# Attention scores as one native float32 product instead of three products of two-part splits

## The chip, the cores and the metric

The kernel runs on one core of a Trainium2 chip. It has five engines with a queue of instructions each: TensorE (PE, with its weight loads listed as PEld), VectorE (DVE), ScalarE (ACT), GpSimd (POOL) and SyncE (SP, which only issues transfers). An engine works through its queue in order; engines wait for each other by semaphores. The metric is the device time of one execution in microseconds (us).

## The reference

Three stages follow each other, all in float32, for 2 sequences of 768 tokens. The change is in the first, attention with 8 heads of 64 columns:

```python
scores = scale * np.matmul(q, k.transpose(0, 1, 3, 2))
keep = is_global | is_local          # the first 8 keys, and the last 96 up to the query
scores = np.where(keep, scores + bias, -1e9)
a = np.exp(scores - np.max(scores, axis=-1, keepdims=True))
a = a / (np.sum(a, axis=-1, keepdims=True) + 1e-09)
x = np.matmul(a, v)
```

The second mixes over the sequence by a product of rank 32 (`moe_U`, `moe_V`) and runs a two-layer channel network with 2048 hidden columns. The third sends each token to one of 8 experts (512 to 1024 to 512) and weights the result. The weights of the second stage come as float64.

## The kernel before, in words

Attention works on 16 heads (2 sequences of 8), two heads (a pair) in the two halves of the 128 partitions. A head has 6 steps, one for each 128 queries, so there are 96 steps, z = 0 to 95. A step's window of keys is 256 columns wide: the local ones and a copy of the first 32.

TensorE multiplies in two ways here. For a tile of type float32r an instruction is one pass over the columns. A product of plain float32 tiles (native, here `values`) is one instruction in the program, and shows as two records in the profile, each with its own weight load. In order to get float32 accuracy from passes, q and k are split into a high part and the rest: kh and kl, qh and ql. `scores` (line 344) then adds three products: kh qh, kl qh, kh ql (lines 351 to 353). A head's q stands in its own half of the partitions and zeros in the other half, so the other head's keys drop out of the sum.

`split_pair` (line 124) makes these parts: for k a cast (line 133) and a subtraction (line 134), for q a cast (139) and a subtraction (140). The first pair is split in two halves of columns ahead of the loop, k on VectorE and q on ScalarE and GpSimd. Each later pair is split while the one before it runs, at the 3rd, 5th and 7th of that pair's 12 steps (`SPLITS`, counted from 0), k's subtraction and both of q's on GpSimd. `load_pair` (line 101) brings raw q and k for a pair, one buffer each, from step 8 of the pair two before on.

A step z is put into the queues in this order: the scores of z; the transposes of step z - 3 (line 376) and their copy on ScalarE (378); the softmax of z, that is one instruction on VectorE that adds the bias and gives the row minimum m (line 363) and an exponential on ScalarE (367); the value products of step z - 6 (392 to 395). There are two score buffers, so the scores of z wait until VectorE is through with those of z - 2. At a head's end VectorE divides by the sums (399 to 401).

One further piece of work is put into the queues with each step, in a fixed order by z (`bg`, `fill`): constants of the mixing stage, then the conversion of the first channel weights from float64 (`from_f64`, lines 230 to 237: four VectorE instructions, one a step), and from step 55 on the mixing product and the transposes of the first sequence. GpSimd also makes a head's bias (line 213, for five of the heads). SyncE issues the transfers in program order; it stops at one whose buffer isn't free.

After step 54 all engines pass a branch around the general form of attention (`other_windows`), and again after the loop. Then come the channel products and the experts, which the change doesn't touch.

Of the kernel before, what the change touches and what calls it, by code (L numbers as in the profile page):

```python
# [22 lines left out]
P = 128  # L23
# [14 lines left out]
# smallest normal float32, as the square of a float64's high word read as float32  # L38
# [3 lines left out]
# positions: the rest of the expert with two tiles or more so far, then the others by falling  # L42
# count in this order; tiles of tokens for each, more are taken at the end
# [9 lines left out]
SPLITS = (3, 5, 7)  # L53
BG0, BGR, SM0 = 6, 8, 6
# columns of the routing's tables
# [9 lines left out]
def tile_kernel(ctx, tc, q, k, v, nn, U, V, w12, wg, wgt, ew, masks, lst0, out, dbg=None):  # L65
# [24 lines left out]
    # ---------------------------------------------------------------- attention: loads  # L90
# [8 lines left out]
    raw_t, qk_t = {}, {}  # L99

    def load_pair(n, parts=1):
        """two heads, one in each half of the partitions"""
        b, h = heads[2 * n]
        if n == 0:
            qr, kr = (x_all[1][:, c:c + 2].rearrange("p a d -> p (a d)")[:, :w] for c, w in ((1, S), (3, NT * 160)))
        else:
            qr = ap.tile([P, S], F32, tag="qr", bufs=1, name=f"qr{n}")
            kr = ap.tile([P, NT * 160], F32, tag="kr", bufs=1, name=f"kr{n}")
        for c in range(parts):
            for t, src in ((kr, k), (qr, q)):  # L110
                w = t.shape[1] // parts
                nc.sync.dma_start(t[:, c * w:c * w + w], src[b, h:h + 2].rearrange("h d s -> (h d) s")[:, c * w:c * w + w])
        raw_t[n] = qr, kr

    # columns: 1, first head, second head, 1; the ones give the sums of the weights
# [5 lines left out]
    # q's parts of one head, zeros in the other head's half of the partitions  # L121
    q_parts = [[[ap.tile([P, S], F32R, name=f"q{w}{j}{r}", bufs=1) for w in "hl"] for j in range(2)] for r in range(2)]

    def split_pair(n, parts=1):
        """q and k in two parts each, whose products sum to float32's"""
        qr, kr = raw_t.pop(n)
        qs = q_parts[n % 2]
        kh = ap.tile([P, NT * 160], F32R, tag="kh", name=f"kh{n}")
        kl = ap.tile([P, NT * 160], F32R, tag="kl", name=f"kl{n}")
        qk_t[n] = qs, kh, kl  # L130
        def k_part(c):
            kc = slice(c * NT * 160 // parts, (c + 1) * NT * 160 // parts)
            nc.vector.tensor_copy(kh[:, kc], kr[:, kc])  # L133
            (nc.vector if parts > 1 else nc.gpsimd).tensor_tensor(kl[:, kc], kr[:, kc], kh[:, kc].bitcast(F32), ALU.subtract)  # L134

        def q_part(c, j):
            qc, r = slice(c * S // parts, (c + 1) * S // parts), slice(D * j, D * j + D)
            hi, lo = qs[j][0][r, qc], qs[j][1][r, qc]
            (nc.scalar.copy if parts > 1 or j == 1 else nc.vector.tensor_copy)(hi, qr[r, qc])
            nc.gpsimd.tensor_tensor(lo, qr[r, qc], hi.bitcast(F32), ALU.subtract)  # L140

        k_part(0)
        q_part(0, 0)
        yield
        for c in range(1, parts):
            k_part(c)
            q_part(c, 0)
            yield
        for c in range(parts):
            q_part(c, 1)  # L150
            yield

    # ---------------------------------------------------------------- constants
# [5 lines left out]
    nc.scalar.dma_start(msk, masks[:, P:7 * P])  # L159
    one_act = const.tile([1, 1], F32, name="one_act")  # L160
    nc.gpsimd.memset(one_act, 0.0)
    nc.scalar.activation(one_act, one_act, AF.Exp)
    nc.sync.dma_start(ident, masks[:, :P])
# [5 lines left out]
    for t in q_parts[0][0]:  # L169
        nc.vector.memset(t[D:].bitcast(F32), 0.0)  # L170
# [3 lines left out]
    first_split = split_pair(0, 2)  # L174
    run(first_split)

    for t in q_parts[1][0]:
        nc.scalar.copy(t[D:], q_parts[0][0][0][D:].bitcast(F32))
# [11 lines left out]
    def distance(dst, is_l, is_g, t, rel, gidx):  # L190
        """dst: the distance where kept, 0 elsewhere; t: 1 where kept"""
        nc.vector.tensor_scalar(is_l, rel, 0.0, None, ALU.is_ge)
        nc.vector.scalar_tensor_tensor(is_l, rel, nlf, is_l, ALU.is_lt, ALU.mult)
        nc.vector.tensor_scalar(is_g, gidx, ngf, None, ALU.is_lt)
        nc.vector.tensor_tensor(t, is_l, is_g, ALU.max)
        nc.vector.tensor_tensor(is_g, t, is_l, ALU.subtract)
        nc.vector.tensor_tensor(dst, rel, is_l, ALU.mult)
        nc.vector.scalar_tensor_tensor(dst, is_g, nlf, dst, ALU.mult, ALU.add)

    # the distance, far where masked; a head's bias is -8 x its slope x this  # L200
# [15 lines left out]
    run(first_split)  # L216
    for t in q_parts[0][1]:
        nc.gpsimd.memset(t[:D].bitcast(F32), 0.0)
    drain(first_split)
    for r in range(2):  # L220
        for c in (0, P + 1):
            nc.gpsimd.memset(v_two[r][:, :, c:c + 1], 1.0)
    for t in q_parts[1][1]:
        nc.gpsimd.memset(t[:D].bitcast(F32), 0.0)

    def from_f64(dst, sq, raw):
        """dst (float32) from the words of float64 in raw [p, n, 2]; below float32's range: zero"""
# [12 lines left out]
    # ---------------------------------------------------------------- weights of the channel products  # L240
    # room for the two parts of two chunks: two of them in "hl"; the float64 words' place, later a third; a fourth at the end
# [39 lines left out]
    # ---------------------------------------------------------------- mixing constants  # L281
# [33 lines left out]
    # routing constants  # L315
# [19 lines left out]
    # ---------------------------------------------------------------- attention: steps  # L335
# [8 lines left out]
    def scores(z):  # L344
        n, i = steps[z]
        k0 = 32 if i == 0 else 160 * (i - 1) + 64
        qs, kh, kl = qk_t[n // 2]
        qh, ql = qs[n % 2]
        c, kc = slice(P * i, P * i + P), slice(k0, k0 + 256)
        s = psa.tile([P, 512], F32, tag="s", bufs=2, name=f"s{z}")  # L350
        nc.tensor.matmul(s[:, :256], qh[:, c], kh[:, kc], start=True, stop=False)  # L351
        nc.tensor.matmul(s[:, :256], qh[:, c], kl[:, kc], start=False, stop=False)  # L352
        nc.tensor.matmul(s[:, :256], ql[:, c], kh[:, kc], start=False, stop=True)  # L353
# [49 lines left out]
    def whole_rows(b, gp):  # L403
        """attention over whole rows, for any n_global and n_local"""
# [66 lines left out]
    # ---------------------------------------------------------------- mixing over the sequence  # L471
    ut = {}

    def mixing(b):
        """x + V'(U'x), in parts: U's and x's first, then those of V and of the product"""
# [49 lines left out]
    # ---------------------------------------------------------------- attention: the loop  # L525
# [6 lines left out]
    spl = first_split  # L532
    for z in range(total + LAGV):
        if z < total:
# [7 lines left out]
            if z == 1:  # L542
                drain(spl)
            if i == 1 and 0 < n + 1 < H:
                head_bias(n + 1)
            if zz == SPLITS[-1] + 1 and n // 2 + 2 < len(heads) // 2:
                drain(spl)
                load_pair(n // 2 + 2)
            if zz in SPLITS and n // 2 + 1 < len(heads) // 2:
                if zz == SPLITS[0]:  # L550
# [854 lines left out]
```

## Time and profile before

| | |
|---|---|
| median of 3 runs | 671.55 us (668.97 to 677.45) |
| span of the profiled execution, first to last instruction | 671.4 us |
| TensorE / VectorE / ScalarE / GpSimd busy | 608.3 / 452.8 / 305.8 / 206.3 us |
| score products, first and last start of line 351 | 8.0 and 144.8 us |
| mean granted TensorE clock | 0.957 of full |

The profiled execution's own time is its span of 671.4 us; no other time was taken of it. Busy time counts what an engine executes, not what it waits for, and overlapping matmuls once. The granted clock is 1.00 (2.4 GHz) or 0.50 (1.2 GHz) at a moment; numbers between are means over a stretch.

### The profile page before, as it was taken

What the parts mean: (1) busy time and instruction counts of PE and PEld (TensorE: products, weight loads), DVE (VectorE), ACT (ScalarE), POOL (GpSimd) and SP (SyncE); (2) the same over time, 40 slices, a digit from 0 to 9 for tenths busy, and PEclk for the clock granted to TensorE, in tenths of its full rate; (3) what the DMA queues carried; (4) which work ended last, traced back from release to release, by engine and by line L of the source; (5) the groups of instructions that cost most, each with busy time, mean ns of one, the idle gap of its engine ahead of it and who ended that gap; (6) DMA issues with size and microseconds to landing.
All of it is one profiled execution on the core that took longest, in us unless ns stands there. A gap on an engine that the chain in (4) does not pass through costs nothing. (4 is left out here: it accounts for less than half of the span.)

```text
span 671.4 us, 10019 instructions
## 1 busy us (share of the span) xinstructions
PE 608.3 (91%) x3568; PEld 541.6 (81%) x3568; DVE 452.8 (67%) x1001; ACT 305.8 (46%) x644; POOL 206.3 (31%) x143
## 2 busy tenths in 40 slices
PE   5989768987998999999999799798989999999991
PEld 3888767986887999989998688776778988889891
DVE  7888959755888887145999651756663568685840
ACT  4766656864333333233222121632353567585830
POOL 4755425602033333223333352502351124031101
PEclk8987978998999999999999899899899999999997
DMA  9632635200333230033010001716257485967300
GB/s 247 226 99 91 213 112 197 65 3 3 125 126 126 93 131 27 0 126 126 32 48 1 0 2 56 289 47 142 95 183 304 146 278 175 364 257 287 125 12 27
DMA packets 35801, 84.08 MB, mean 125 GB/s; under 512 B 5567, under 2 KB 17727, under 8 KB 33680
## 3 DMA queue, kind: packets, MB, share of 16 engines
q1 hardware_dynamic: 31568, 71.52, 31.2%
q0 software_dynamic: 2784, 7.09, 3.0%
q10 hardware_dynamic: 1376, 4.59, 1.8%
q8 instruction: 33, 0.54, 0.4%
q14 instruction: 40, 0.33, 0.2%
HBM read 75.32 MB, written 8.77 MB: 125 GB/s over the span
## 5 line engine op out<-in xcount | busy, mean ns | idle before, releaser
L609 ACT ACTIVATE hh<-g 128x384 fp32r<-128x384 f32 x62 | 30.4, 490 | 115.0 <-PE g L606 114.6
L610 DVE SCALAR_TENSOR_TENSOR hl<-g,hh 128x384 fp32r<-128x384 f32 x62 | 34.2, 554 | 51.8 <-ACT hh L609 51.5
L367 ACT ACTIVATE e<-t,m 128x256 f32<-128x256 f32 (+1 forms) x96 | 47.3, 493 | 31.4 <-DVE m L363 30.6
L351 PE MATMUL s<-kh,qh 128*128 128x256 f32 x96 | 38.0, 396 | 23.6 <-DVE m L363 17.5
L848 POOL DMA_INDIRECT out_dram<-x,ids x13 | 13.1, 1008 | 123.8 <-ACT x L847 100.2
L363 DVE CUSTOM_DVE_ANT_0 t<-s,bias 128x256 f32<-128x256 f32 (+1 forms) x96 | 37.4, 394 | 17.9 <-PE s L353 11.5
L677 DVE CUSTOM_DVE_ANT_0 sq_w<-x,wgt 128x512 f32<-128x512 f32 x54 | 46.3, 857 | 1.4
L230 ACT ACTIVATE sq_w<-w 128x512 f32<-128x512 f32 x32 | 21.5, 671 | 49.7 <-DVE wf L237 49.7
L351 PEld LDWEIGHTS s<-kh,qh 128*128 128x128 f32 x96 | 20.5, 214 | 27.8 <-DVE m L363 21.4
L378 ACT COPY et<-pt 128x256 f32<-128x256 f32 (+1 forms) x96 | 33.2, 347 | 13.6 <-PE pt L376 12.8
L376 PE MATMUL pt<-ident,e 128*128 128x128 f32 x176 | 38.0, 292 | 0.0
L235 DVE SCALAR_TENSOR_TENSOR wf<-w,wf 128x512 int32<-128x512 int32 x32 | 35.2, 1100 | 0.8
L134 POOL TENSOR_TENSOR kl<-kr,kh 128x960 fp32r<-128x960 f32 x7 | 21.6, 3081 | 43.8 <-DVE kh L133 25.4
L395 PE MATMUL o<-v,et 128*128 128x65 f32 x160 | 33.6, 295 | 0.0
L768 POOL DMA_INDIRECT lst<-tab,slot x12 | 12.8, 1063 | 65.7 <-DVE tab L764 31.3
L233 DVE SCALAR_TENSOR_TENSOR wf<-w,wf 128x512 int32<-128x512 int32 x32 | 29.0, 908 | 4.6 <-issue 4.1
L610 DVE SCALAR_TENSOR_TENSOR ehlr<-egr,ehhr 128x256 fp32r<-128x256 f32 x28 | 11.9, 425 | 26.8 <-ACT ehhr L609 26.8
L353 PE MATMUL s<-kh,ql 128*128 128x256 f32 x96 | 29.4, 306 | 0.0
L352 PE MATMUL s<-kl,qh 128*128 128x256 f32 x96 | 29.4, 306 | 0.0
L394 PE MATMUL o<-v,et 128*128 128x65 f32 x160 | 29.0, 266 | 0.0
L140 POOL TENSOR_TENSOR ql<-qr,qh 64x768 fp32r<-64x768 f32 x14 | 26.9, 1918 | 1.4 <-POOL ql L140 1.0
L395 PEld LDWEIGHTS o<-v,et 128*128 128x128 f32 x160 | 27.0, 211 | 0.0
(777 smaller groups left out, 2150.4 us busy)
## 6 DMA issues: line engine op xcount, KB each, us to landing
ew<-in_ew_dram SPq DMA_DIRECT2D x32, 1024.0 KB, 7.5
w<-in_w_dram SPq DMA_DIRECT2D x16, 1024.0 KB, 4.8
v<-in_v_dram SPq DMA_DIRECT2D x8, 704.0 KB
ew<-in_ew_dram ACTq DMA_DIRECT2D x4, 1024.0 KB, 14.3
kr<-in_k_dram SPq DMA_DIRECT2D x7, 480.0 KB
x2d<-x SPq DMA_DIRECT2D x12, 256.0 KB
qr<-in_q_dram SPq DMA_DIRECT2D x7, 384.0 KB, 3.0
wgt<-in_wgt_dram SPq DMA_DIRECT2D x4, 512.0 KB, 3.6
```

The lines of the kernel that those rows point to most:

```text
L235: nc.vector.scalar_tensor_tensor(t, high, -0x40000000, t, ALU.bitwise_and, ALU.bitwise_or)
L351: nc.tensor.matmul(s[:, :256], qh[:, c], kh[:, kc], start=True, stop=False)
L352: nc.tensor.matmul(s[:, :256], qh[:, c], kl[:, kc], start=False, stop=False)
L353: nc.tensor.matmul(s[:, :256], ql[:, c], kh[:, kc], start=False, stop=True)
L363: nc.vector.tensor_tensor_reduce(out=t[:, :w], in0=s[:, :w], in1=bias[:, h, b0:b0 + w], scale=-0.125, scalar=3.0e38, op0=ALU.add, op1=ALU. ...
L367: nc.scalar.activation(e[:, :w], t[:, :w], AF.Exp, bias=m, scale=-1.0)
L376: nc.tensor.transpose(pt[:, c0:c0 + P], e[:, c0:c0 + P], ident)
L378: nc.scalar.copy(et[:, :w], pt[:, :w])
L395: nc.tensor.matmul(oo, et[:, P:256], vt[:, i, vc], start=False, stop=True)
L609: nc.scalar.activation(hi, src, AF.Relu)
L610: nc.vector.scalar_tensor_tensor(lo, src, 0.0, hi.bitcast(F32), ALU.max, ALU.subtract)
L677: nc.vector.tensor_tensor_reduce(out=sq_w, in0=x_t[0, i], in1=rooms[k % 2][:, DM * j:DM * j + DM], scale=1.0, scalar=0.0, op0=ALU.mult, op ...
```

## The change

Raw k goes into `kt`, two buffers in turn, and q straight into two tiles for each of two pairs in turn, a head's 64 rows in its half of the partitions; the other half is cleared once at the start. Both stay plain float32. `scores` is one native product. `split_pair`, the four part tiles and `SPLITS` are gone. A pair's loads are now issued at the second step of the pair before it (in the first pair's case at the start, as before), in three transfers instead of two. The transfer of the identity moves from SyncE's queue to ScalarE's, and the ones beside v are written earlier. Comments are removed, so line numbers differ.

```diff
-    raw_t, qk_t = {}, {}
+    qk_t = {}
+    q_two = [[ap.tile([P, S], F32, name=f"q{j}{r}", bufs=1) for j in range(2)] for r in range(2)]
+    def q_zero(r, engine):
+        for j in range(2):
+            engine.memset(q_two[r][j][D * (1 - j):D * (1 - j) + D], 0.0)
     def load_pair(n, parts=1):
         b, h = heads[2 * n]
-        ...
-                nc.sync.dma_start(t[:, c * w:c * w + w], src[b, h:h + 2].rearrange("h d s -> (h d) s")[:, c * w:c * w + w])
-        raw_t[n] = qr, kr
+        kt = ap.tile([P, NT * 160], F32, tag="kt", bufs=2, name=f"kt{n}")
+        qk_t[n] = q_two[n % 2], kt
+        def k_part(c):
+            w = NT * 160 // parts
+            nc.sync.dma_start(kt[:, c * w:c * w + w], k[b, h:h + 2].rearrange("h d s -> (h d) s")[:, c * w:c * w + w])
+        def q_part(j, c):
+            w = S // parts
+            nc.sync.dma_start(q_two[n % 2][j][D * j:D * j + D, c * w:c * w + w], q[b, h + j, :, c * w:c * w + w])
+        for j in range(2):
+            for c in range(parts):
+                if j == 0:
+                    k_part(c)
+                q_part(j, c)
-    q_parts = ...
-    def split_pair(n, parts=1):
-        ...
     warm = x_all[1][:, 0].bitcast(BF16)[:, 0:512]
     nc.vector.memset(warm, 1.0)
-    for t in q_parts[0][0]:
-        nc.vector.memset(t[D:].bitcast(F32), 0.0)
+    q_zero(0, nc.vector)
+    q_zero(1, nc.gpsimd)
+    for r in range(2):
+        for c in (0, P + 1):
+            nc.gpsimd.memset(v_two[r][:, :, c:c + 1], 1.0)
...
-    first_split = split_pair(0, 2)
-    run(first_split)
...
     head_bias(0)
-    run(first_split)
-    ...
-        qs, kh, kl = qk_t[n // 2]
-        qh, ql = qs[n % 2]
+        qs, kt = qk_t[n // 2]
         c, kc = slice(P * i, P * i + P), slice(k0, k0 + 256)
         s = psa.tile([P, 512], F32, tag="s", bufs=2, name=f"s{z}")
-        nc.tensor.matmul(s[:, :256], qh[:, c], kh[:, kc], start=True, stop=False)
-        nc.tensor.matmul(s[:, :256], qh[:, c], kl[:, kc], start=False, stop=False)
-        nc.tensor.matmul(s[:, :256], ql[:, c], kh[:, kc], start=False, stop=True)
+        nc.tensor.matmul(s[:, :256], qs[n % 2][:, c], kt[:, kc], start=True, stop=True)
...
-            if zz == SPLITS[-1] + 1 and n // 2 + 2 < len(heads) // 2:
-                drain(spl)
-                load_pair(n // 2 + 2)
-            if zz in SPLITS and n // 2 + 1 < len(heads) // 2:
-                if zz == SPLITS[0]:
-                    spl = split_pair(n // 2 + 1)
-                run(spl)
+            if zz == 1 and n > 1 and n // 2 + 1 < len(heads) // 2:
+                load_pair(n // 2 + 1)
```

Three places in the engines' queues. First VectorE, from the last instructions of the distance to the first softmaxes (t and m; s is the score buffer). Before:

```order
L206 SCALAR_TENSOR_TENSOR dist<-msk,nf,dist 128x384
L213 TENSOR_SCALAR bias<-dist 128x384
L133 CAST kh_134<-x_69 128x480
L134 TENSOR_TENSOR kl_135<-x_69,kh_134 128x480
L363 ISA t_186,m_187<-s_182,bias 128x128
L363 ISA m_187 128x1
```

and now:

```order
L185 SCALAR_TENSOR_TENSOR dist<-msk,nf,dist 128x384
L192 TENSOR_SCALAR bias<-dist 128x384
L330 ISA t_165,m_166<-s_163,bias 128x128
L330 ISA m_166 128x1
L330 ISA t_173,m_174<-s_171,bias 128x256
```

The first softmax now follows the bias directly; the second half of k's split no longer stands between them.

Second GpSimd, from the first whole pair's split on. Before:

```order
L134 TENSOR_TENSOR kl_211<-kr_107,kh_210 128x960
L140 TENSOR_TENSOR ql_89<-qr_106,qh_88 64x768
L140 TENSOR_TENSOR ql_91<-qr_106,qh_90 64x768
L332 MEMSET route_180 40x256
L332 MEMSET route_181 40x256
L213 TENSOR_SCALAR bias<-dist 128x384
L134 TENSOR_TENSOR kl_448<-kr_308,kh_447 128x960
L140 TENSOR_TENSOR ql_85<-qr_307,qh_84 64x768
L140 TENSOR_TENSOR ql_87<-qr_307,qh_86 64x768
```

and now, up to the last bias:

```order
L302 MEMSET route_161 40x256
L302 MEMSET route_162 40x256
L192 ISA
L192 TENSOR_SCALAR bias<-dist 128x384 x4
L282 TENSOR_TENSOR vst<-v_418,vst 32x768
L192 TENSOR_SCALAR bias<-dist 128x384
```

The subtractions are gone; the five bias products and one constant remain of GpSimd's work in attention.

Third SyncE, from the routing tables' transfer (tab) on; kr, qr, kt and q are k and q of a pair, w the float64 weights. Before:

```order
L330 DMA tab<-in_masks_dram 128x133
L112 DMA kr_308<-in_k_dram 128x960
L112 DMA qr_307<-in_q_dram 128x768
L252 DMA w_0_0_383<-in_w_dram 128x2048
L252 DMA w_0_1_385<-in_w_dram 128x2048
```

and now:

```order
L300 DMA tab<-in_masks_dram 128x133
L222 DMA w_0_0_328<-in_w_dram 128x2048
L222 DMA w_0_1_330<-in_w_dram 128x2048
L115 DMA kt_356<-in_k_dram 128x960
L119 DMA q_82<-in_q_dram 64x768
L119 DMA q_83<-in_q_dram 64x768
```

Pair 2's k and q have moved behind the first two weight transfers.

## Rows read from the trace of the kernel before

**Rows 1.** The page: busy us, share of the span, instructions, by engine.
```profile
PE 608.3 (91%) x3568; PEld 541.6 (81%) x3568; DVE 452.8 (67%) x1001; ACT 305.8 (46%) x644; POOL 206.3 (31%) x143
```
**Rows 2.** Stretches, line 351 alone: length, busy (x count), granted clock, DMA share, GB/s.
```profile
14.60:20.10 5.50, 2.72 (x5) 1.53 (x5) 0.50 0.89 217
20.10:30.35 10.25, 3.67 (x10) 1.91 (x10) 1.00 0.76 288
30.35:41.00 10.65, 2.65 (x6) 1.42 (x6) 0.84 0.50 157
46.80:58.20 11.40, 3.04 (x6) 1.62 (x6) 0.70 0.46 141
63.00:72.30 9.30, 1.89 (x5) 0.94 (x5) 1.00 0.44 133
72.30:79.65 7.35, 2.61 (x7) 1.33 (x7) 1.00 0.51 196
96.00:102.25 6.25, 1.57 (x5) 0.95 (x5) 1.00 0.28 100
102.25:119.80 17.55, 3.68 (x9) 2.23 (x10) 0.81 0.53 175
```
**Rows 3.** Waits, 0 to 150 us: who waited for whom, us, times, longest.
```profile
PE s L351 <- DVE m L363: 17.5, 16, 5.6
```
**Rows 4.** Timeline, 63.6 to 68 us: start, length, instruction, [idle before, releaser].
```profile
63.64 3.58 POOL L134 TENSOR_TENSOR kl<-kr,kh 128x960 fp32r<-128x960 f32 x1 [3.38 <-PE pt L376]
...
65.17 2.33 DVE L231 TENSOR_SCALAR wf<-w 128x512 int32<-128x512 int32 x1
...
67.90 0.39 PE L351 MATMUL s<-kh,qh 128*128 128x256 f32 x1 [1.51 <-DVE m L363]
```
**Rows 5.** Line 231: count, shortest/median/longest ns, first to last start.
```profile
L231 DVE TENSOR_SCALAR wf<-w x32: 415/420/2333, 60.6 to 263.6; 128x512 int32<-128x512 int32 x32
```
**Rows 6.** Timeline of TensorE, one quiet step, 60.05 to 61.11 us.
```profile
60.08 0.36 PE L351 MATMUL s<-kh,qh 128*128 128x256 f32 x1
...
60.52 0.38 PE L376 MATMUL pt<-ident,e 128*128 128x128 f32 x2
60.74 0.33 PE L394 MATMUL o<-v,et 128*128 128x65 f32 x2
...
61.10 0.36 PE L351 MATMUL s<-kh,qh 128*128 128x256 f32 x1
```
**Rows 7.** Groups by line, GpSimd, 0 to 160 us: busy us, mean ns, idle before.
```profile
L140 POOL TENSOR_TENSOR ql<-qr,qh 64x768 fp32r<-64x768 f32 x14 | 26.9, 1918 | 1.4 <-POOL ql L140 1.0
L134 POOL TENSOR_TENSOR kl<-kr,kh 128x960 fp32r<-128x960 f32 x7 | 21.6, 3081 | 43.8 <-DVE kh L133 25.4 <-PE pt L376 17.1 <-PE s L353 1.3
```
**Rows 8.** Timeline of VectorE and TensorE, 9.4 to 14.7 us.
```profile
9.49 2.41 DVE L213 TENSOR_SCALAR bias<-dist 128x384 f32<-128x384 f32 x1
...
14.30 0.28 DVE L363 CUSTOM_DVE_ANT_0 t<-s,bias 128x128 f32<-128x128 f32 x1
...
14.64 0.58 PE L351 MATMUL s<-kh,qh 128*128 128x256 f32 x1 [5.55 <-DVE m L363]
```
**Rows 9.** Stretch at the low clock, line 351 alone; columns as in rows 2.
```profile
89.30:94.85 5.55, 1.70 (x3) 0.97 (x4) 0.50 0.52 163
```
**Rows 10.** Four lines of products; columns as in rows 5 (394 and 705: native).
```profile
L351 PE MATMUL s<-kh,qh x96: 277/366/583, 8.0 to 144.8; 128*128 128x256 f32 x96
L394 PE MATMUL o<-v,et x160: 220/275/423, 20.8 to 148.5; 128*128 128x65 f32 x160
L705 PE MATMUL lp<-wg_sb,x x24: 172/257/257, 445.8 to 465.6; 128*128 128x9 f32 x24
L604 PE MATMUL z<-er_0h,ehhr x22: 388/398/505, 529.6 to 641.7; 128*128 128x512 f32 x22
```
**Rows 11.** Timeline of TensorE, 532.3 to 533.1 us: passes of 512 columns.
```profile
532.46 0.40 PE L604 MATMUL z<-er_0h,ehhr 128*128 128x512 f32 x1
...
532.93 0.39 PE L606 MATMUL z<-er_0h,ehlr 128*128 128x512 f32 x1
```

More of the change, by code (lines that the diff above doesn't have):

```diff
@@ L52 @@
 PA, PB = 'ab', 'abcd'
-SPLITS = (3, 5, 7)
 BG0, BGR, SM0 = 6, 8, 6
@@ L98, in tile_kernel @@
     heads = [(b, h) for b in range(B) for h in range(H)]
-    raw_t, qk_t = {}, {}
+    qk_t = {}
[3 more added lines that the diff above has]
+            engine.memset(q_two[r][j][D * (1 - j):D * (1 - j) + D], 0.0)
     def load_pair(n, parts=1):
         b, h = heads[2 * n]
[L104 to L111, printed above, removed]
-                nc.sync.dma_start(t[:, c * w:c * w + w], src[b, h:h + 2].rearrange("h d s -> (h d) s")[:, c * w:c * w + w])
-        raw_t[n] = qr, kr
+        kt = ap.tile([P, NT * 160], F32, tag="kt", bufs=2, name=f"kt{n}")
[11 more added lines that the diff above has]
+                q_part(j, c)
     v_two = [ap.tile([P, 2 * NT - 1, P + 2], F32, name=f"v{r}", bufs=1) for r in range(2)]
@@ L119, in load_v @@
         nc.sync.dma_start(v_two[n % 2][:, :, 1:P + 1], v[n // (H // 2), n % (H // 2)])
-    q_parts = [[[ap.tile([P, S], F32R, name=f"q{w}{j}{r}", bufs=1) for w in "hl"] for j in range(2)] for r in range(2)]
-    def split_pair(n, parts=1):
[L126 to L151, printed above, removed]
     nraw = const.tile([P, 4], I32, name="nraw")
@@ L159, in tile_kernel @@
     nc.scalar.dma_start(msk, masks[:, P:7 * P])
+    nc.scalar.dma_start(ident, masks[:, :P])
     one_act = const.tile([1, 1], F32, name="one_act")
@@ L162, in tile_kernel @@
     nc.scalar.activation(one_act, one_act, AF.Exp)
-    nc.sync.dma_start(ident, masks[:, :P])
     relf, gidf = msk[:, 0:384], msk[:, 384:768]
@@ L173, in tile_kernel @@
         nc.tensor.matmul(wp_, warm[:, 0:P], warm, start=True, stop=True)
-    first_split = split_pair(0, 2)
-    run(first_split)
-    for t in q_parts[1][0]:
-        nc.scalar.copy(t[D:], q_parts[0][0][0][D:].bitcast(F32))
     io = dict(allow_small_or_imprecise_dtypes=True)
@@ L215, in tile_kernel @@
     head_bias(0)
-    run(first_split)
[L217 to L224, printed above, removed]
     def from_f64(dst, sq, raw):
@@ L531, in tile_kernel @@
     fill = []
-    spl = first_split
     for z in range(total + LAGV):
@@ L541, in tile_kernel @@
                 load_w1(0, 1)
-            if z == 1:
-                drain(spl)
             if i == 1 and 0 < n + 1 < H:
                 head_bias(n + 1)
-            if zz == SPLITS[-1] + 1 and n // 2 + 2 < len(heads) // 2:
-                drain(spl)
-                load_pair(n // 2 + 2)
-            if zz in SPLITS and n // 2 + 1 < len(heads) // 2:
-                if zz == SPLITS[0]:
-                    spl = split_pair(n // 2 + 1)
-                run(spl)
+            if zz == 1 and n > 1 and n // 2 + 1 < len(heads) // 2:
+                load_pair(n // 2 + 1)
             s = scores(z)
```

## The prediction

> **What bounds the kernel now.** I read the page first: TensorE is busy for 608.3 us, 91% of the span, so what it does or waits for sets the time [rows 1]. But the change touches only the attention stage, the first 145 us. So I cut that stage into stretches and counted score steps in each, by the first score product, line 351 [rows 2]. There are two kinds. Quiet stretches, 20.10 to 30.35 and 72.30 to 79.65, hold 10 + 7 steps in 17.6 us, 1.035 us a step. Disturbed ones hold 6, 6 and 5 steps in 10.65, 11.40 and 9.30 us, nearly twice that. The wait list says what TensorE lacks: 17.5 us before line 351 until VectorE's row minimum (m, line 363) frees a score buffer [rows 3].
>
> The timeline of one disturbed stretch shows why VectorE is late [rows 4]. GpSimd subtracts kl from 63.64 for 3.58 us. VectorE begins a step of the weight conversion, line 231, at 65.17, and it ends only after that subtraction: 2.33 us for an instruction whose median is 0.42 [rows 5]. Behind it in VectorE's queue stands the next softmax, and TensorE idles 1.51 us. I read this as VectorE being held by GpSimd's splits, not as too much work on VectorE.
>
> TensorE's own step in a quiet place takes 1.02 us (60.08 to 61.10): three score products 0.44, two transposes 0.22, two value products 0.36 [rows 6].
>
> **The change, part by part.** *Splits removed.* GpSimd loses 7 subtractions of k (21.6 us) and 14 of q (26.9) [rows 7], beside the small ones of the first pair; VectorE and ScalarE lose the casts before them. What this gives is counted at TensorE. Four stretches in which GpSimd subtracts stand in [rows 2]. At 1.035 us a step the first three would take 6.21, 6.21 and 5.18, so they lose 4.4, 5.2 and 4.1. The fourth, 102.25 to 119.80, also runs the mixing product; the undisturbed mixing stretch before it, from 96.00, takes 6.25 for 5 steps, so its nine steps are worth 11.25 of 17.55 and 6.3 is lost. Sum: **20.0 us**. Part of it is the clock that falls behind the stalls (0.84, 0.70 and 0.81 granted there); it returns with them. I leave the stop between 82 and 96 us as it is: it falls at the branch to the general form of attention, which the change doesn't touch.
>
> *Start.* VectorE begins the first head's bias (line 213) at 9.49 and needs 2.41 us for it, under GpSimd's clearing and subtracting; then it splits the second half of k, and the first softmax starts only at 14.30 [rows 8]. By line 231, which is longer, such an operation undisturbed takes at most 0.42 [rows 5]. Without the split the softmax would follow it: 4.81 - 0.42 = 4.4 us go. Nor does TensorE stand idle for 5.55 us, behind which its next five steps took 5.50 us at a granted clock of 0.50 [rows 2, 8]. Steps at that clock take 1.85 us (three in 5.55) [rows 9], so at full clock these five would need 5.50 x 1.035 / 1.85 = 3.1. I take 2.1 us off, not 2.4, since they also wait on softmaxes. Start: **6.5 us**.
>
> *The score product.* 96 times, three passes of 256 columns become one native product, which the program's native value products show as two records each. No row has a native product of 256 columns. Lower bound: two halves at today's mean of 0.44 / 3 = 0.147 a pass, 0.29, a gain of 0.15 x 96 = 14 us. Upper bound: each half streams its columns twice and then shows a weight load as well. Three rows decide [rows 10]. A native half with 9 columns lasts 0.172 us at least, one with 65 columns 0.220: 0.86 ns a column. With 256 columns that makes 0.220 + 191 x 0.00086 = 0.384, and a plain pass of 512 columns lasts 0.388 at least. So a native half of 256 columns is like a pass of 512, and two of these follow each other in 0.47 us [rows 11]. That is 0.47 against 0.44 a score product, **+3 us** over 96. As to weight loads: four native halves of 65 columns, each with its own load, take 0.36 us, 0.09 each [rows 6], though their columns are few. If such a load were not hidden under 256 columns either, a product would cost 0.47 + 0.18 = 0.65, +20 us. I take it as hidden, as the loads of the passes in rows 11 are.
>
> The Trainium skill (FP8 and Floating Point Precision, section TensorE Precision Notes) speaks against the change: a true float32 product takes four passes through the array, against three here. By that rule, at today's 0.147 a pass, the product would cost 0.59, the term would be +14 and the time 661. The trace agrees on the four (two halves at twice the time a column), not on the price.
>
> *Loads and zeros.* Two halves of q are cleared on VectorE before data comes, as now, the others earlier on GpSimd. SyncE issues three transfers a pair instead of two, and no longer waits for splits before them. But it moves pair 2's k and q behind the first two transfers of weights, 1 MB each. All that is issued early keeps the DMAs near full until about 20 us (share 0.89 from 14.60) [rows 2]; from there they move 288 GB/s at a share of 0.76, so 379 when full, and 2.1 MB of weights and 0.9 MB of pair 2 take 8 us more: landed at 28 to 29. Pair 2 is needed at step 24: step 2 at about 9.2, five short steps of 3 us, 17 at 1.035: 30. A tie, so **+1 us** (0 to 4).
>
> *What is late next.* GpSimd's five bias products stay, and hold VectorE as its splits did, mostly where little is converted: **+1 us** (0 to 5). VectorE's conversions are next: the quiet stretch from 72.30 is full of them, at 1.05 us a step, and it is in my nominal step already. So where TensorE's longer product falls beside them it costs less than counted.
>
> **Sum.** -20.0 - 6.5 + 3 + 1 + 1 = -21.5 on the profiled span of 671.4: 649.9. The runs' median, 671.55, is 0.15 above: 650 us. What comes after 145 us is only moved forward.
>
> **Rivals.**
> 1. *The clock stays low (slower).* Attention's matrix work would be native products and transposes alone. If these don't hold the granted clock up, steps cost 1.85 instead of 1.035: 0.81 x 96 = +78 us, less the 26 of waits that vanish: 723. It turns the result from 21.5 / 0.81 = 27 such steps on. Against: values and transposes are already 0.58 of the 1.02 us, and the clock is 1.00 in the quiet stretches. For: no stretch shows them alone. The Trainium skill (TensorE: Matmul & The Clock Gate, section Part 4: PE-mode transpose) says that transposes don't count as activity for the clock; no row here tests it. 6%.
> 2. *Weight loads show:* 0.65 a product, 17 us over my term: 667, no change. 7%.
> 3. *Something else holds VectorE,* say the transfers that run in the same stretches. Then the start is gained, and of the 20.0 perhaps half, through the casts that are gone: 660. Against: line 231 ended with GpSimd's subtraction, and the quiet stretch from 72.30 has a DMA share of 0.51, above the 0.44 of the disturbed one before it [rows 2]. 12%.
> 4. *A native half is a single pass:* -14 instead of +3, but only where VectorE isn't itself at its limit, about half of the steps: 640. Against: the durations by column. 9%.
>
> **Chances.** My case 66%, from 640 to 659 with the bounds of its terms. The runs before spread from 668.97 to 677.45, so about 2% can be told from no change: the line is 658.1. Faster: nearly all of my case, rival 4 and a third of rival 3: 77%. Within 2%: 16%. Slower: 7%. The range 635 to 664 takes in my case and rivals 3 and 4; 1, 2 and the tails are left out.
>
> **What would show it.** First softmax at 9 to 10 us; conversions over 1 us only beside the bias products; GpSimd nearly idle until the channel weights are split; score halves 0.23 to 0.24 apart; the last score product near 123 us instead of 144.8 [rows 10]; the length from there to the end unchanged. I am wrong if halves lie over 0.3 apart, if the clock in attention reads 0.5, or if conversions still take 2 us while GpSimd is idle.

## The result and the profile after

The changed kernel takes 651.36 us in the median of 4 runs (649.48 to 655.39), the one before 670.76 beside it (4 runs): a ratio of 0.969 [0.966, 0.973]. The forecast was 650. The profiled execution has a span of 647.7 us against 671.4. It is the fastest of the four, and its own time, 649.48, lies 1.8 us above its span. With the same 1.8 the execution that was profiled before would be one of 673.2 (an estimate), 2.4 above its median. So of the 23.7 us between the two spans the medians confirm 19.4, and what is read below from the two traces adds up to some 4 us more than the runs gained.

The page, busy time by engine (answers [rows 1]):

```profile
PE 601.1 (93%) x3472; PEld 527.9 (82%) x3472; DVE 423.1 (65%) x983; ACT 297.5 (46%) x631; POOL 150.6 (23%) x116
```

TensorE still bounds the kernel. GpSimd is busy for 55.7 us less, VectorE for 29.7. TensorE is busy for only 7.2 us less, so 16.5 of the 23.7 us came from time in which it had stood idle.

The score products by stretches, now line 320, with the same steps of the program as in [rows 2] (length, busy, weight loads busy, granted clock, DMA share, GB/s; a product is two records, so 12 are 6 steps):

```profile
12.70:24.75 12.05, 6.55 (x20) 3.04 (x21) 1.00 1.09 294
24.75:31.00 6.25, 3.90 (x12) 1.81 (x12) 1.00 1.04 300
37.30:43.55 6.25, 3.90 (x12) 1.81 (x13) 1.00 0.42 119
48.70:54.10 5.40, 3.30 (x10) 1.51 (x10) 1.00 0.22 63
54.10:61.70 7.60, 4.60 (x14) 2.16 (x15) 1.00 0.95 295
84.65:96.30 11.65, 5.68 (x18) 3.21 (x19) 1.00 0.61 201
```

The four disturbed stretches of [rows 2] (10.65, 11.40, 9.30 and 17.55 us) are the second, third, fourth and sixth row: 4.4, 5.15, 3.9 and 5.9 us shorter, 19.35 together. The clock in them is 1.00 instead of 0.84, 0.70, 1.00 and 0.81. The two quiet ones grew, from 10.25 to 12.05 and from 7.35 to 7.60.

What TensorE waited for up to 125 us (answers [rows 3]; the columns are who, for whom, us in total, times, longest; "issue" is a wait for which the profile shows no cause):

```profile
PE s L320 <- issue: 6.3, 1, 6.3
PE s L320 <- DVE m L330: 2.1, 2, 1.3
```

The 17.5 us behind the row minimum are 2.1. What is left over is one stop of 6.3 us, at the branch after step 54, which was 5.92 long in the trace before (the profile names a conversion as what ended it there).

The start (answers [rows 8]):

```profile
8.32 0.36 DVE L192 TENSOR_SCALAR bias<-dist 128x384 f32<-128x384 f32 x1
8.38 1.35 POOL L192 TENSOR_SCALAR bias<-dist 128x384 f32<-128x384 f32 x1 [5.32 <-DVE dist L185]
8.83 0.29 DVE L330 CUSTOM_DVE_ANT_0 t<-s,bias 128x128 f32<-128x128 f32 x1 [0.15 <-DVE bias L192]
...
9.18 0.48 PE L320 MATMUL s<-kt,q 128*128 128x256 f32 x1 [0.87 <-DVE m L330]
```

The first bias takes 0.36 us on VectorE instead of 2.41, the first softmax starts at 8.83 instead of 14.30, and TensorE stands for 0.87 us instead of 5.55. VectorE's bias began before GpSimd's this time.

One conversion line over the whole kernel (answers [rows 5]), GpSimd's bias products, now its costliest group up to 123 us (answers [rows 7]), and the score products (answers [rows 10]):

```profile
L201 DVE TENSOR_SCALAR wf<-w x32: 415/419/500, 46.0 to 241.3; 128x512 int32<-128x512 int32 x32
```

```profile
L192 POOL TENSOR_SCALAR bias<-dist 128x384 f32<-128x384 f32 x5 | 6.0, 1209 | 5.5 <-DVE dist L185 5.3
```

```profile
L320 PE MATMUL s<-kt,q x192: 377/379/794, 7.3 to 122.9; 128*128 128x256 f32 x192
```

The longest conversion of this line is 0.50 us; it was 2.33. The hold itself is still in the kernel, only later: beside GpSimd's splits of the channel weights, from 136 us on, conversions of line 205 take up to 2.78 us. A native half lasts 0.379, as forecast (0.384). The last one starts at 122.9, against 144.8 for the last score before. From there to the end it is 524.8 us against 526.6, so the gain lies in attention.

A quiet step of TensorE (answers [rows 6]):

```profile
31.06 0.65 PE L320 MATMUL s<-kt,q 128*128 128x256 f32 x2
31.55 0.38 PE L343 MATMUL pt<-ident,e 128*128 128x128 f32 x2
31.77 0.34 PE L361 MATMUL o<-v,et 128*128 128x65 f32 x2
31.94 0.39 PE L362 MATMUL o<-v,et 128*128 128x65 f32 x2
32.16 0.67 PE L320 MATMUL s<-kt,q 128*128 128x256 f32 x2
```

It is 1.10 us long, where it was 1.02. From the score to the transposes it is 0.49 us, before 0.44; most of the rest is added just ahead of the score, where the last value product took 0.08 us to the score's start and now takes 0.11. Compared step by step, most undisturbed steps are 0.07 to 0.08 us longer.

One new wait appeared, in the first quiet stretch:

```profile
16.73 0.26 DVE L201 TENSOR_SCALAR u_f<-u_raw 128x192 int32<-128x192 int32 x1 [2.75 <-DMA u_raw<-in_moe_U_dram]
...
17.39 0.48 PE L320 MATMUL s<-kt,q 128*128 128x256 f32 x1 [1.28 <-DVE m L330]
```

VectorE waits 2.75 us for the transfer of U, the softmax stands behind it, and TensorE loses 1.28.

### The profile page after: what moved, and what is told of

Its sections match the earlier page's. It is cut to its first block, busy times and chain, and to the rows that moved or that the text cites. A ratio compares the mean times of both kernels' runs of the same rounds, so it can differ in the third digit from the quotient of the medians.

```text
span 647.7 us, 9752 instructions
## 1 busy us (share of the span) xinstructions
PE 601.1 (93%) x3472; PEld 527.9 (82%) x3472; DVE 423.1 (65%) x983; ACT 297.5 (46%) x631; POOL 150.6 (23%) x116
## 5 line engine op out<-in xcount | busy, mean ns | idle before, releaser
L320 PE MATMUL s<-kt,q 128*128 128x256 f32 x192 | 62.5, 410 | 8.7 <-issue 6.3
L334 ACT ACTIVATE e<-t,m 128x256 f32<-128x256 f32 (+1 forms) x96 | 47.2, 492 | 15.8 <-DVE m L330 14.9
L330 DVE CUSTOM_DVE_ANT_0 t<-s,bias 128x256 f32<-128x256 f32 (+1 forms) x96 | 38.1, 399 | 20.4 <-PE s L320 10.4
L200 ACT ACTIVATE sq_w<-w 128x512 f32<-128x512 f32 x32 | 21.5, 672 | 49.7 <-DVE wf L207 49.7
L320 PEld LDWEIGHTS s<-kt,q 128*128 128x128 f32 x192 | 30.9, 195 | 11.0 <-issue 6.5
L343 PE MATMUL pt<-ident,e 128*128 128x128 f32 x176 | 35.5, 276 | 0.0
L205 DVE SCALAR_TENSOR_TENSOR wf<-w,wf 128x512 int32<-128x512 int32 x32 | 32.5, 1016 | 0.8
L343 PEld LDWEIGHTS pt<-ident,e 128*128 128x128 f32 x176 | 25.0, 144 | 8.8 <-issue 0.4
L362 PE MATMUL o<-v,et 128*128 128x65 f32 x160 | 31.4, 279 | 0.0
L203 DVE SCALAR_TENSOR_TENSOR wf<-w,wf 128x512 int32<-128x512 int32 x32 | 27.3, 852 | 5.8 <-issue 5.4
L569 DVE SCALAR_TENSOR_TENSOR ehlr<-egr,ehhr 128x256 fp32r<-128x256 f32 x28 | 11.9, 425 | 26.8 <-ACT ehhr L568 26.2
L361 PE MATMUL o<-v,et 128*128 128x65 f32 x160 | 27.3, 253 | 0.0
L727 POOL DMA_INDIRECT lst<-tab,slot x12 | 11.9, 990 | 65.4 <-DVE tab L723 27.7
L361 PEld LDWEIGHTS o<-v,et 128*128 128x128 f32 x160 | 24.7, 195 | 1.1
L362 PEld LDWEIGHTS o<-v,et 128*128 128x128 f32 x160 | 24.8, 196 | 0.0
L568 ACT ACTIVATE ehhr<-egr 128x256 fp32r<-128x256 f32 x28 | 10.8, 385 | 29.9 <-PE egr L565 29.9
L207 DVE SCALAR_TENSOR_TENSOR wf<-sq_w,wf 128x512 f32<-128x512 f32 x32 | 22.0, 688 | 1.3
```

Of the source, the lines that this page charges most:

```text
L203: nc.vector.scalar_tensor_tensor(t, low, 29, t, ALU.logical_shift_right, ALU.bitwise_or)
L205: nc.vector.scalar_tensor_tensor(t, high, -0x40000000, t, ALU.bitwise_and, ALU.bitwise_or)
L320: nc.tensor.matmul(s[:, :256], qs[n % 2][:, c], kt[:, kc], start=True, stop=True)
L330: nc.vector.tensor_tensor_reduce(out=t[:, :w], in0=s[:, :w], in1=bias[:, h, b0:b0 + w], scale=-0.125, scalar=3.0e38, op0=ALU.add, op1=ALU. ...
L334: nc.scalar.activation(e[:, :w], t[:, :w], AF.Exp, bias=m, scale=-1.0)
L343: nc.tensor.transpose(pt[:, c0:c0 + P], e[:, c0:c0 + P], ident)
```

## The experiments

Ratios are to the kernel before, in runs on the same chip. A difference in us between two of them is the difference of their ratios times 671; by their intervals such a difference is uncertain by 3 to 5 us.

**1. GpSimd's subtractions back, run when they like.** Added to the changed kernel, at steps 3 and 5 of a pair:

```diff
+        if zz == 3:
+            nc.gpsimd.tensor_tensor(scr_k, kt, kt, ALU.subtract)
+            nc.gpsimd.tensor_tensor(scr_q[:D], qs[0][:D], qs[0][:D], ALU.subtract)
+        if zz == 5:
+            nc.gpsimd.tensor_tensor(scr_q[D:], qs[1][D:], qs[1][D:], ALU.subtract)
```

> The changed kernel with GpSimd's subtractions put back alone: for each of the first seven pairs one of 128x960 and two of 64x768, of k and q into scratch that nothing reads; no casts, scores stay native. Theory (VectorE is held by GpSimd): the stalls come back: conversions of over 1 us beside the subtractions, waits of TensorE on VectorE's m, 15 to 25 us more than the changed kernel's 651.4, so 666 to 676. Rival (VectorE's and ScalarE's own casts, or the transfers, made the stalls): within 3 us of 651.4, conversions stay at 0.42 and 0.69 us.

Measured: 659.89 us (657.43 to 661.62), ratio 0.982 [0.976, 0.988], 8.5 us above the changed kernel. That is below my range and above the rival's. The waits for the row minimum came back only in part:

```profile
PE s L320 <- DVE m L330: 7.0, 9, 2.8
```

Nothing tied these subtractions to their step, so several ran at the start or in the stop at the branch, and they read one operand twice and were shorter (1.79 us for k). The test was not yet the work that had been removed.

**2. The casts back, without subtractions.** Two casts on VectorE at step 3, one on ScalarE at step 5:

```diff
+        if zz == 3:
+            nc.vector.tensor_copy(scr_k, kt)
+            nc.vector.tensor_copy(scr_q[:D], qs[0][:D])
+        if zz == 5:
+            nc.scalar.copy(scr_q[D:], qs[1][D:])
```

> The changed kernel with the other half of the split put back alone: for seven pairs a cast of 128x960 and one of 64x768 on VectorE and one of 64x768 on ScalarE, into scratch; GpSimd does nothing more. Theory (held by GpSimd): 1.2 us more work of VectorE a pair, mostly beside TensorE: 0 to 5 us more than 651.4. Rival (VectorE's own work made the stalls): 12 to 25 us more.

Measured: 652.83 us (651.66 to 653.99), ratio 0.971 [0.966, 0.976], 1 us above the changed kernel by the ratios, though 4.7 us later at the last score of the two traces. That is in my range and far from the 12 to 25 us of the rival: the casts alone didn't make the stalls.

**3. The subtractions held to their step and in their old form.**

```diff
+        if zz == 3:
+            nc.vector.tensor_copy(kh[:, 0:1], kt[:, 0:1])
+            nc.gpsimd.tensor_tensor(kl, kt, kh.bitcast(F32), ALU.subtract)
+            nc.vector.tensor_copy(qh[:D][:, 0:1], qs[0][:D][:, 0:1])
+            nc.gpsimd.tensor_tensor(ql[:D], qs[0][:D], qh[:D].bitcast(F32), ALU.subtract)
...
```

> The changed kernel with GpSimd's subtractions put back into scratch tiles (nothing reads the results), this time with the operands and formats of the kernel before (plain float32 minus a float32r tile) and held to the 3rd and 5th step of each pair by a cast of one column ahead of each. The casts of whole tiles stay out. Theory (GpSimd's subtractions lengthen VectorE's conversions beside them, and those hold the softmax): subtractions of 2 to 4.5 us each as before, conversions of 1 to 2.8 us beside them, TensorE's waits for the row minimum up by 10 to 18 us, and the time 662 to 672, above the 659.9 of the kernel whose subtractions ran when they liked. Rival (the stalls needed the whole casts on VectorE as well): 655 to 661. Rival (the subtractions cost nothing, and the earlier 8.5 us came from where they happened to fall): 651 to 654.

Measured: 666.06 us (664.10 to 669.11), ratio 0.993 [0.990, 0.996]: 15.8 us above the changed kernel and within 2% of the kernel before. The time is in my range and in neither rival's. The waits for the row minimum were 2.1 us in the changed kernel and are now

```profile
PE s L320 <- DVE m L330: 10.5, 11, 2.1
```

That is 8.4 us more, less than the 10 to 18 that I had expected. Most of the rest is the clock: it reads 0.50 in four stretches of attention, 20.4 us together, where the changed kernel has one of 6.8. The 13.6 us more at half speed are worth some 6.8 (an estimate). One place of the trace, GpSimd, VectorE and TensorE in order of time:

```profile
54.30 2.22 POOL L502 TENSOR_TENSOR scr_kl<-kt,scr_kh 128x960 fp32r<-128x960 f32 x1 [2.43 <-DVE scr_qh L503]
...
54.57 2.50 DVE L207 SCALAR_TENSOR_TENSOR wf<-sq_w,wf 128x512 f32<-128x512 f32 x1
...
56.48 2.28 POOL L504 TENSOR_TENSOR scr_ql<-q,scr_qh 64x768 fp32r<-64x768 f32 x1
56.99 0.41 DVE L330 CUSTOM_DVE_ANT_0 t<-s,bias 128x256 f32<-128x256 f32 x1
...
57.34 1.71 DVE L201 TENSOR_SCALAR wf<-w 128x512 int32<-128x512 int32 x1
...
57.47 0.70 PE L320 MATMUL s<-kt,q 128*128 128x256 f32 x2 [0.69 <-DVE m L330]
```

The conversion at 54.57 starts 0.27 us after the subtraction and ends at 57.07, 0.55 after the subtraction's end; undisturbed it takes 0.69. So it stood until the subtraction was through and ran then. All twelve conversions of this trace that begin during one of these subtractions end behind it, by 0.1 to 0.6 us. The next subtraction, from 56.48, in turn takes 2.28 us, where the median of its line is 1.97. The conversion at 57.34 repeats it. But the softmax between them, at 56.99, runs beside a subtraction and takes its usual 0.41. All softmax instructions of this kernel:

```profile
L330 DVE CUSTOM_DVE_ANT_0 t<-s,bias x96: 276/417/425, 8.9 to 138.5; 128x256 f32<-128x256 f32 x80, 128x128 f32<-128x128 f32 x16
```

The longest is 0.425, as it is without any subtraction (0.426 in the changed kernel). The Trainium skill (SBUF — State Buffer, section Who interferes with whom) says that VectorE and GpSimd share one pair of ports as an exclusive lock, that a VectorE instruction with two SBUF inputs contends with GpSimd's reads, and that one with at most one SBUF input doesn't unless it runs in a two-port mode. The trace agrees on the conversion at 54.57, which has two SBUF inputs and stood, and on the softmax, which reads its scores from PSUM and never did. The one at 57.34 has one SBUF input (0.42 us undisturbed) and stood too; whether it ran in a two-port mode no run shows.

**4. The whole split back.** As before, with full casts in place of those of one column; the score stays one native product.

```diff
+        if zz == 3:
+            nc.vector.tensor_copy(kh, kt)
...
+            nc.vector.tensor_copy(qh[:D], qs[0][:D])
...
+        if zz == 5:
+            nc.scalar.copy(qh[D:], qs[1][D:])
...
```

> The changed kernel with the whole split of pairs 0 to 6 put back at the 3rd and 5th steps, casts on VectorE and ScalarE and subtractions on GpSimd, into scratch that nothing reads; the score stays one native product. If the splits account for the 20.0 us of my sum and the native product costs about 0.07 us a step, the four disturbed stretches come back nearly whole and the time is 668 to 675, though the early start stays. If casts and subtractions together cost no more than they do apart (1 + 8.5), it is 659 to 663.

Measured: 668.64 us (665.21 to 670.61), ratio 0.995 [0.992, 0.998], 17.2 us above the changed kernel and within 2% of the kernel before. It is in the first range; in its trace the last score product starts at 144.2 instead of 122.9. The waits:

```profile
PE s L320 <- DVE m L330: 13.0, 18, 1.4
```

So the splits of later pairs are worth 17.2 us in the runs' times and 21.3 in the attention stage of this trace. By the runs some 16 of the 17 are GpSimd's subtractions (3) and one or so the casts (2), each within 3 to 4 us. The 3.3 us that are left to the kernel before are small, as the early start and the dearer product nearly cancel. With the whole casts back GpSimd is slowed in its turn: a subtraction of k takes up to 4.92 us here (4.82 in the kernel before), where it took at most 2.24 in 3, and conversions beside that long one run in their usual 0.68.

**5. The subtractions moved to VectorE, in the kernel before.** The three products stay; only pair 0's q is still subtracted on GpSimd.

```diff
-            (nc.vector if parts > 1 else nc.gpsimd).tensor_tensor(kl[:, kc], kr[:, kc], kh[:, kc].bitcast(F32), ALU.subtract)
+            nc.vector.tensor_tensor(kl[:, kc], kr[:, kc], kh[:, kc].bitcast(F32), ALU.subtract)
...
-            nc.gpsimd.tensor_tensor(lo, qr[r, qc], hi.bitcast(F32), ALU.subtract)
+            (nc.gpsimd if parts > 1 else nc.vector).tensor_tensor(lo, qr[r, qc], hi.bitcast(F32), ALU.subtract)
```

> The kernel before, with the subtractions of k and q of pairs 1 to 7 on VectorE instead of GpSimd: some 2.8 us more work on VectorE a pair, none on GpSimd; scores stay three products. Theory (held by GpSimd): faster than before although the engine that TensorE waits for gets more work: 655 to 666 against 670.8. Rival (VectorE has too much to do): slower than before, 674 to 690.

Measured: 691.70 us (689.02 to 692.26), ratio 1.028 [1.022, 1.033]. I had put it on the wrong side, and it is even above the rival's 690. The conversions were short, as the theory says (line 231 at most 0.66 us), but the third step of a pair had become this on VectorE:

```profile
70.12 0.65 DVE L133 CAST kh<-kr 128x960 fp32r<-128x960 f32 x1
70.81 1.16 DVE L134 TENSOR_TENSOR kl<-kr,kh 128x960 fp32r<-128x960 f32 x1
71.88 0.55 DVE L139 CAST qh<-qr 64x768 fp32r<-64x768 f32 x1
72.46 0.95 DVE L140 TENSOR_TENSOR ql<-qr,qh 64x768 fp32r<-64x768 f32 x1
73.34 0.41 DVE L363 CUSTOM_DVE_ANT_0 t<-s,bias 128x256 f32<-128x256 f32 x1
...
73.81 0.58 PE L351 MATMUL s<-kh,qh 128*128 128x256 f32 x1 [2.50 <-DVE m L363]
```

3.2 us of VectorE's queue stand in one block ahead of a softmax, and TensorE has work for two steps only. I had counted VectorE's total and not the block. Waits for the row minimum were 26.7 us, more than the 17.5 of [rows 3]. The subtractions no longer lengthened other work, but now stood in the way themselves.

**6. The product's price.** Two kernels add work to each score of the changed one, once three passes on tiles of zeros, once a second native product on a q of zeros:

```diff
+        for last in (False, False, True):
+            nc.tensor.matmul(s[:, :256], zq[:, c], zk, start=False, stop=last)
```

```diff
+        nc.tensor.matmul(s[:, :256], zq[:, c], kt[:, kc], start=False, stop=True)
```

> The changed kernel with three passes of 256 columns on zeros added to each score product, which changes no sum; it prices today's three products after a native one. In quiet steps (1.10 us now) 0.35 to 0.44 more by the kernel before's steps. Read with the next such run, that adds a native product on zeros instead: if the native one costs 0.47 (loads hidden) to 0.49 (one load of the two shows) its step is 0.03 to 0.13 longer than this one's; if a native half were a single pass, 0.1 shorter.

> The changed kernel with a second native product of 128 x 256 added to each score, on a q tile of zeros. With both weight loads of a native product hidden a step grows by 0.43 us (two halves of 0.216), with one of them showing by 0.49, with both showing by 0.54; three plain passes added the same way grew it by 0.36. So a native product for three passes costs 0.07, 0.13 or 0.18 us a step by this; the traces of the two kernels, product for product, gave 0.07 to 0.08.

Measured, one run each: 681.07 and 687.82 us, with spans of 679.2 and 686.0. One quiet step, first with the passes added, then with the native product:

```profile
39.71 0.65 PE L325 MATMUL s<-kt,q 128*128 128x256 f32 x2
40.01 0.71 PE L327 MATMUL s<-zk,zq 128*128 128x256 f32 x3
40.55 0.38 PE L350 MATMUL pt<-ident,e 128*128 128x128 f32 x2
...
41.17 0.43 PE L325 MATMUL s<-kt,q 128*128 128x256 f32 x1
```

```profile
41.26 0.65 PE L323 MATMUL s<-kt,q 128*128 128x256 f32 x2
41.75 0.59 PE L324 MATMUL s<-kt,zq 128*128 128x256 f32 x2
42.18 0.38 PE L347 MATMUL pt<-ident,e 128*128 128x128 f32 x2
...
42.79 0.43 PE L323 MATMUL s<-kt,q 128*128 128x256 f32 x1
```

The steps are 1.46 and 1.53 us, against 1.10. Three passes cost 0.36, 0.12 each; a native product 0.43, no weight load showing. Its price over three passes is 0.07 a step, 6.7 us over 96; the spans, of one run each, differ by 6.8. The first native product of the step takes 0.49 (41.26 to 41.75), 0.06 more than the second. In steps 5 and 6 of the changed kernel, where transposes alone stand ahead of the score, it takes 0.44 and 0.45. So what comes first behind the narrow value products pays some 0.05, and the 0.44 of [rows 6], against 0.36 for three passes, held such a surcharge too.

**7. Two small edits to gain more.** A head's first step multiplies the 128 columns that are used, and U is fetched early on ScalarE's queue:

```diff
-        nc.tensor.matmul(s[:, :256], qs[n % 2][:, c], kt[:, kc], start=True, stop=True)
+        w = width(i)
+        nc.tensor.matmul(s[:, :w], qs[n % 2][:, c], kt[:, k0:k0 + w], start=True, stop=True)
...
+    nc.scalar.dma_start(u_raw.rearrange("p n two -> p (n two)"), U.bitcast(I32))
```

> The changed kernel with two small edits: the first step of a head, whose softmax reads 128 of the 256 columns, multiplies only those (16 of 96 products), and the transfer of U is issued first of all on ScalarE's queue, so that the conversion of U no longer waits 2.75 us for it at 13.98 us. If half the columns halve the two halves' streams, 16 times about 0.21 us is saved, 3.4, and the wait for U cost TensorE 1.28: 645.5 to 648.5 beside 651.4. If VectorE sets the step there, or the early transfer delays q and k of the first pair by as much, 650 to 652.

Measured: 648.71 us (644.68 to 649.27), ratio 0.964 [0.961, 0.968], 3.4 us below the changed kernel by the ratios. As a difference that is in my range, as a time a hair above it; it is not told apart from the changed kernel's 0.969. Its trace shows both gains until step 23, and then this:

```profile
32.98 0.46 PE L321 MATMUL s<-kt,q 128*128 128x128 f32 x2 [2.35 <-DMA q<-in_q_dram]
```

The third pair's q comes late, behind the two weight transfers. Behind the stop the granted clock read 0.50 from 33.4 to 36.9 us, in steps 25 and 26.

**8. The third pair ahead of the weights,** with the two edits of 7:

```diff
-            if n == 2 and i == 0:
+            if n == 2 and i == 2:
                 load_w1(0, 0)
                 load_w1(0, 1)
```

> The two edits of the kernel before this one (128 columns in a head's first step, U early) and a third: the first two transfers of channel weights are issued behind the third pair's k and q instead of ahead of them, as in the kernel before the change. In the trace of the two edits alone the gain was there until step 23 (1.7 us ahead of the changed kernel) and was lost at step 24, where the score waited 2.35 us for q, which landed at 32.85 us behind 2 MB of weights, and steps 25 and 26 ran at half the clock (1.45 us more). If the order of these transfers is the cause, that wait goes, the gain stays and grows by 0.21 us a head: 3.8 us less than the two edits alone, about 643 to 646. If something else of the early part stops it there, 647 to 650.

Measured: 648.63 us (646.18 to 651.69), ratio 0.9625 [0.959, 0.966]. In attention it did what was expected:

```profile
30.38 0.44 PE L321 MATMUL s<-kt,q 128*128 128x128 f32 x2
```

Step 24 waits for nothing, and the last score starts at 119.0 instead of 122.9. But the span is 646.7, only 1.0 us less than the changed kernel's. As a time it lies in the range of "something else", as a difference (4.6 us below the changed kernel, by the ratios) between the two; of the 3.8 us that I had expected over experiment 7 the ratios show 1.3. About 1.5 us is given back in the channel stage: in both kernels TensorE waits 3.43 us there for VectorE, and behind it the clock falls, in this one for longer. Eight us from that wait's end, TensorE alone (length, busy, granted clock, DMA share, GB/s), first the changed kernel, then this one:

```profile
351.70:359.70 8.00, 7.96 (x35) 0.79 0.00 0
```

```profile
348.30:356.30 8.00, 7.94 (x27) 0.59 0.00 0
```

At 0.59 instead of 0.79 these 8 us do 0.20 x 8 = 1.6 us less work at full clock. Product for product, the lead over the changed kernel is 3.4 us ahead of that wait and 1.9 behind it; the rest goes in smaller pieces. No edit touches that place; whether the clock does so in every run the profiles can't say. This is the fastest kernel here that keeps the general form; its interval and the changed kernel's, [0.966, 0.973], just meet, so its 4.6 us are at the edge of what these runs can tell.

**9. Without the branch.** From the changed kernel, and from that of 8, one line is taken out:

```diff
-            other_windows(0)
```

> The changed kernel without the branch around the general form of attention after step 54 (its code for the first sequence is left out; for these masks it is never entered). If the stop of TensorE by 6.34 us and the steps at half the clock behind it are due to that branch, 8 to 10 us go: 641 to 644. If the stop has another cause that only shows there, 650 to 652.

> The kernel with the three edits, and without the branch around the general form of attention after step 54 (left out for the first sequence, never entered for these masks). If the two gains are independent, another 9 us, as taking it out of the changed kernel gave: 634 to 637. If the work that fills the stop today comes back as a wait elsewhere, 638 to 643.

Measured: 642.25 us (641.68 to 643.44), ratio 0.956 [0.953, 0.960], and 641.69 (639.28 to 644.35), ratio 0.953 [0.948, 0.958]. The first is where it was expected, 8.7 us below the changed kernel. In the changed kernel the step behind the branch starts so:

```profile
71.29 1.22 PE L320 MATMUL s<-kt,q 128*128 128x256 f32 x2 [6.34 <-issue]
```

and without the branch so:

```profile
66.52 0.65 PE L320 MATMUL s<-kt,q 128*128 128x256 f32 x2
...
67.39 0.65 PE L320 MATMUL s<-kt,q 128*128 128x256 f32 x2
```

The stop and the slow steps behind it (2.19 and 2.13 us at a clock of 0.50, 1.28 at a mean of 0.77) are gone. In the trace that place alone gives 8.6 us: this kernel is 2.6 behind the changed one up to step 54, since U lands later in it, and 6.0 ahead from step 64 on. The Trainium skill (Runtime: NRT & Kernel Launch, section Instruction fetch mechanics) says that a branch taken out of the fetched window makes an engine wait for its instructions. That fits a wait for which the changed kernel's profile shows no cause; no run shows the fetch itself, or parts the jump from the rest of the construct. The second kernel missed its 634 to 637 and came out in the other range, 638 to 643: its last score starts at 111.0, 11.9 us earlier than in the changed one, but its span is 9.0 less. Product for product its lead is 11.3 us up to 395 us and 8.9 from 470 on, so part is again lost later.

## Why the prediction was right, step by step

**The time** was 650 against 651.36, and the time went where I had said: VectorE is no longer held by GpSimd's splits. One term was off by nearly 4 us, and smaller errors of the opposite sign hid it; that the sum came within 1.4 us is in part luck. I had also set the profiled span of 671.4 equal to the runs' median, though a span lies 1.8 us below its own execution's time; the saving was 21.5 by my sum, 19.4 by the medians and 23.7 by the spans.

- *Splits, -20.0.* Right in size and cause. The four stretches lost 19.35 us, and their 26 steps carry 0.07 us more each, so 21.2 was gained in this pair of traces. Put back whole, the splits cost 17.2 us by the times and 21.3 in attention (experiment 4). That it is GpSimd's subtractions, and not the casts or the transfers, follows from 2 and 3; rival 3 is out.
- *Start, -6.5.* The first softmax came 5.5 us earlier, not 4.4 (0.7 of it is already there at the first score), and the five steps behind it took 1.9 us less, not 2.1, at a clock of 1.00. The ten steps of the quiet stretch begin at 12.70 instead of 20.10 [rows 2]: 7.4.
- *The score product, +3.* **This term was mis-sized: 6.8.** The half was as forecast, 0.38 long; the two follow each other in 0.27 us behind the value products and in 0.22 elsewhere (forecast 0.23 to 0.24). I went wrong on the other side of the comparison: I took [rows 6]'s 0.44 for three passes, though it holds the surcharge behind the value products, which stays. Three passes cost 0.36, a native product 0.43 (experiment 6). I had set 0.47 against 0.44; like for like it is 0.43 against 0.36, and from the score's start to the transposes, where only part of it shows, 0.49 against 0.44. Rivals 2 and 4 are out: no weight load shows, and a half is no single pass. The four passes of the Trainium skill (FP8 and Floating Point Precision, section TensorE Precision Notes) agree with it: 0.43 / 4 = 0.108 each, close to the 0.12 of a float32r pass. I had priced them at 0.147, which is why I called them right in number and wrong in price.
- *Loads, +1 (0 to 4).* The tie at step 24 was real, and closer than I had it: in the changed kernel q lands at 32.02 us by the trace's semaphores, not at 28 to 29, and the step starts at 32.16, not at 30, without a wait. In experiment 7, where the steps before it ran 1.7 us earlier and q landed at 32.85, it cost 2.35. What came late instead was U, which I had not looked at: 1.28 us.
- *Late next, +1 (0 to 5).* Conversions of line 201 reach 0.50 us at most, so the five bias products cost next to nothing; the steps outside the four stretches even gained some 1.1 us beside what the product and U cost them. The largest stop left is the branch's, which I had left where it was: 6.34 us, and 8.7 with what follows (experiment 9).
- *The clock* (rival 1). It is 1.00 in all of attention but 69.4 to 76.2 us, at and behind the stop at the branch. No run here has transposes alone, so what the Trainium skill says of them (TensorE: Matmul & The Clock Gate, section Part 4: PE-mode transpose) no run here shows.

Sum by what the two traces show: 7.4 + 21.2 + 1.1 gained, 1.3 lost to U and 6.2 to the dearer product (0.07 in the 88 steps behind the start), 22.2 at the end of attention by the first half of the last score (144.8 to 122.6). The 1.1 is what the sum leaves over. The remaining 1.5 of the span's 23.7 lie behind attention and belong to no edit.

Where I failed was in experiments: 5 by sign, 1 in size, and 8 and 9 by believing that what is gained in attention arrives at the end.

## What to carry to other kernels

Work that is moved to an idle engine can cost more on the engine it spares: look for instructions of an unusual length, and see whether they end just behind one of GpSimd's. Moving it back isn't free either; a block of 3 us in a queue that feeds TensorE every 1.1 us is a stall, however idle the engine is on average. Price a replaced instruction by what its removal gives, from like places on both sides, not by the time from its start to the next thing.

## What the runs showed of the hardware

- In experiment 3 every conversion on VectorE that begins during a GpSimd subtraction ends behind it (0.69 became 2.50 us, 0.42 became 1.71); the softmax, which reads PSUM and one SBUF tile, isn't held (0.425 at most). The hold goes both ways: a subtraction of 2.24 us became 4.92 where whole casts ran on VectorE (experiment 4).
- A native float32 product of 128 x 256 costs 0.43 us at full clock, three float32r passes 0.36, and the first native product behind products of 65 columns 0.06 more.
- A branch that is passed and not entered stopped TensorE for 6.3 us, and its clock read 0.50 until 4.9 us behind the stop.
